# Paired softmax inverses, triangles by GpSimd in the second batch, zero matmuls between early steps, and new figures and random turns in the planner of an attention and feed-forward kernel

## The chip, the cores and the metric

One core of a Trainium2 chip runs one program. The metric is the device time of one execution in microseconds (us). PE is the matrix engine, DVE the vector engine, ACT the scalar engine, POOL is GpSimd, SP issues transfers.

## What is computed

```
scores = q @ k.T / 8, kept where key < 4 (sinks) or 0 <= query - key < 128, else -1e9
a   = exp(scores - max);  a = a / (sum(a) + 1e-9)
x   = a @ v, heads side by side                # 4 batches, 8 heads, 768 positions, 64 wide: x is 4 x 768 x 512
u   = x + ((x.T @ U) @ V).T                    # U 768 x 32, V 32 x 768: mixes the positions
out = u + relu(u @ w1) @ w2                    # w1 512 x 2048, w2 2048 x 512
```

q, k and v are fp32 in memory; U, V, w1 and w2 are fp64, which the kernel reads as raw 64-bit words and narrows itself; the two scalars (sinks and window) are integers.

## The kernel before, in words

The work is written as steps (`Plan.add`, `Plan.any`): each has an engine or a choice of engines with a cost in us for each, the buffers it reads and writes, and a priority. When all steps are there, `Plan.order` builds the program's order: `forward` simulates the engines with these costs and hands out steps, `backward` computes new priorities from the end, eleven passes in turn, and the order of the pass that came out shortest by the planner's own figures is emitted. Each engine then runs its instructions strictly in that order; a semaphore wait holds everything behind it on the same engine.

The stages, in the order of the data:

- **Start.** `sink_attention_mixer` (before `Fast`) runs eight matmuls on zeros (`spin`, L1320), loads the two scalars, builds masks on DVE and POOL, and issues the first transfers: q and k of two pairs of heads, and the 64-bit words of U, V (two halves) and the first w1 block into four `big` buffers (L1332).
- **Attention of batches 0 and 1** goes by pairs of heads (`attend_pair`). For each of three blocks of 128 queries and each head PE computes a score block into a bank of PSUM (L652); DVE scales, masks and takes the row minimum of the negated block (`soften`, L704, with an accumulator read); ACT takes the exponential and the row sum (L707). `normalise` adds 1e-9 to the three sums of a head (L715, ACT or DVE, the planner picks), DVE takes the reciprocal (L718), and POOL, ACT or DVE scale the probabilities (L729, L727, L730). PE transposes them (L745); the transposed blocks get two triangles: the part from the previous key block by a DVE multiplication with a mask straight out of PSUM (L754), the own block by a copy (L467 or L468) and a POOL affine_select (L770). PE multiplies with v (L675).
- **Attention of batches 2 and 3** goes head by head (`scores`, `values`), in a split fp32r form; there both triangles are POOL selects (L767 and L770), because `transposes` gets `whole=False`.
- **Mixing**: sums over positions, the product with V, and `u` split into a high and a low part (`uh`, `ul`; L982, L474).
- **Feed-forward** (`ffn`): 16 blocks of 128 hidden units by two halves of 384 positions by four batches. A block is 12 matmuls of 384 columns (L1006, L1007, L1008), a relu (ACT or DVE, `hh`), a low part (`hl`, L1017, DVE), and 9 matmuls of 512 columns (L1027). In batch 0 the weights come in beside it: `weights` narrows each of 32 half blocks by seven operations on DVE, ACT and POOL (`narrow_steps`, L99 to L108), then writes a high part (L467) and a low part (L474, `w`). The attention of the next batch runs beside the feed-forward of this one.

PE, DVE, ACT and POOL take their steps from one list, so one changed cost moves instructions everywhere. Banks of PSUM are a ring of eight: a step that writes a bank waits until all readers of its last content are done.

## Time and profile before

| | us |
|---|---|
| three runs | 753.15, 753.34, 753.82; median 753.34 |
| profiled execution, first to last instruction (its span) | 750.5 |
| between that span and the median of the runs | 2.84 |
| PE busy in the span | 727.3 (97%) |
| DVE, ACT, POOL busy | 454.3, 341.4, 194.0 |

The profile lists the span of the profiled execution and no other time of it; what lies around the span is put at the 2.84 us between it and the median. Busy time of PE is the union of its matmuls, which overlap, so it counts some waiting as work; waits are to be read from the steps between starts.

### The profile page before, as it was taken

What the parts mean: (1) busy time and instruction counts of PE and PEld (TensorE: products, weight loads), DVE (VectorE), ACT (ScalarE), POOL (GpSimd) and SP (SyncE); (2) the same over time, 40 slices, a digit from 0 to 9 for tenths busy, and PEclk for the clock granted to TensorE, in tenths of its full rate; (3) what the DMA queues carried; (4) which work ended last, traced back from release to release, by engine and by line L of the source; (5) the groups of instructions that cost most, each with busy time, mean ns of one, the idle gap of its engine ahead of it and who ended that gap; (6) DMA issues with size and microseconds to landing.
All of it is one profiled execution on the core that took longest, in us unless ns stands there. A gap on an engine that the chain in (4) does not pass through costs nothing.

```text
span 750.5 us, 11587 instructions
## 1 busy us (share of the span) xinstructions
PE 727.3 (97%) x4012; PEld 629.2 (84%) x4012; DVE 454.3 (61%) x1168; ACT 341.4 (45%) x977; POOL 194.0 (26%) x316
## 2 busy tenths in 40 slices
PE   7989999999998999999999999999999999999997
PEld 5557777777787999999899899999999989889895
DVE  7999889798999577667751287675653131112111
ACT  6986475775874445555541164564441111111110
POOL 4652030421521263263510043544401000000000
PEclk9999999999999999999999999999999999999999
DMA  7466758755795378563575468760276536524752
GB/s 261 150 197 226 261 182 302 258 184 205 240 296 223 124 244 278 177 209 117 167 241 183 153 194 256 231 211 1 71 263 227 169 135 237 199 76 138 267 176 96
DMA packets 43780, 146.84 MB, mean 196 GB/s; under 512 B 5440, under 2 KB 12224, under 8 KB 34240
## 3 DMA queue, kind: packets, MB, share of 16 engines
q1 hardware_dynamic: 43424, 145.62, 57.7%
q8 instruction: 33, 0.54, 0.3%
q10 hardware_dynamic: 288, 0.39, 0.2%
q14 instruction: 35, 0.29, 0.1%
HBM read 116.37 MB, written 29.62 MB: 195 GB/s over the span
## 4 chain that ended last, share of the span: by engine, by line
PE 84%; DVE 11%; ACT 1%; issue 1%; DMA 1%; POOL 0%; SPq 0%; DVEq 0%; ACTq 0%
PE bank L1027 33%; PE bank L1006 12%; PE bank L1007 11%; PE bank L1008 11%; PE bank L793 3%; PE bank L745 2%; PE bank L652 2%; PE bank L675 2%; DVE nr L104 2%; PE bank L695 2%; PE bank L696 2%; DVE w L474 1%; DVE bank L106 1%; PE bank L906 1%; DVE p L704 1%
## 5 line engine op out<-in xcount | busy, mean ns | idle before, releaser
L1027 PE MATMUL bank<-w,hh 128*128 128x512 f32 x768 | 246.2, 402 | 1.2 <-ACT hh L1014 0.6
L1017 DVE SCALAR_TENSOR_TENSOR hl<-bank,hh 128x384 fp32r<-128x384 f32 x128 | 70.9, 554 | 186.9 <-ACT hh L1014 186.1
L1006 PE MATMUL bank<-ul,w 128*128 128x384 f32 x512 | 178.5, 349 | 0.8 <-ACT w L467 0.7
L1007 PE MATMUL bank<-uh,w 128*128 128x384 f32 x512 | 174.0, 340 | 1.8 <-DVE w L474 1.8
L1008 PE MATMUL bank<-uh,w 128*128 128x384 f32 x512 | 173.1, 338 | 0.0
L1014 ACT ACTIVATE hh<-bank 128x384 fp32r<-128x384 f32 x121 | 59.3, 490 | 236.6 <-PE bank L1008 235.9
L1027 PEld LDWEIGHTS bank<-w,hh 128*128 128x128 f32 x768 | 139.6, 189 | 24.5 <-issue 1.4
L1027 PE MATMUL bank<-w,hl 128*128 128x512 f32 x384 | 151.8, 395 | 2.3 <-DVE hl L1017 2.3
L1006 PEld LDWEIGHTS bank<-ul,w 128*128 128x128 f32 x512 | 96.3, 188 | 12.1 <-issue 3.4
L1007 PEld LDWEIGHTS bank<-uh,w 128*128 128x128 f32 x512 | 96.4, 188 | 8.6 <-DVE w L474 3.7
L1008 PEld LDWEIGHTS bank<-uh,w 128*128 128x128 f32 x512 | 96.2, 188 | 0.0
L1027 PEld LDWEIGHTS bank<-w,hl 128*128 128x128 f32 x384 | 72.2, 188 | 20.8 <-DVE hl L1017 3.6
L707 ACT ACTIVATE p<-p,ms 128x132 f32<-128x132 f32 (+1 forms) x144 | 69.9, 486 | 33.4 <-DVE ms L704 32.9
L704 DVE CUSTOM_DVE_ANT_0 p<-bank,mask 128x132 f32<-128x132 f32 (+1 forms) x144 | 54.3, 401 | 13.3 <-PE bank L696 10.8
L476 POOL TENSOR_TENSOR p<-p 128x256 f32<-128x256 f32 (+1 forms) x26 | 21.7, 836 | 131.0 <-ACT p L707 130.3
L476 POOL TENSOR_TENSOR ul<-xT,uh 128x384 fp32r<-128x384 f32 x14 | 14.4, 1050 | 146.0 <-ACT uh L467 146.0
L467 ACT COPY tb<-bank 64x384 f32<-64x384 f32 x31 | 14.7, 474 | 40.0 <-PE bank L793 40.0
L729 POOL TENSOR_TENSOR p<-p,r 128x396 f32<-128x396 f32 x27 | 24.2, 898 | 32.4 <-DVE r L718 26.0
L474 DVE TENSOR_TENSOR xT<-bank,tb 64x384 f32<-64x384 f32 x32 | 17.5, 548 | 23.1 <-ACT tb L467 22.8
L770 POOL TENSOR_SCALAR_AFFINE_SELECT oph<-oph 128x384 fp32r<-128x384 f32 (+1 forms) x48 | 27.4, 572 | 12.8 <-ACT oph L467 10.2
L745 PE MATMUL bank<-ident,p 128*128 128x128 f32 x144 | 24.9, 278 | 3.4 <-POOL p L729 2.2
L770 POOL TENSOR_SCALAR_AFFINE_SELECT opl<-opl 128x384 fp32r<-128x384 f32 (+1 forms) x48 | 26.1, 544 | 7.4 <-ACT opl L467 4.1
(187 smaller groups left out, 1137.7 us busy)
## 6 DMA issues: line engine op xcount, KB each, us to landing
w<-wd SPq DMA_DIRECT2D x60, 1024.0 KB, 4.9
big<-in_w_dram SPq DMA_DIRECT2D x32, 512.0 KB, 4.2
wd<-w SPq DMA_DIRECT2D x14, 1024.0 KB, 4.4
big<-xd SPq DMA_DIRECT2D x33, 256.0 KB, 3.2
qkraw<-in_k_dram SPq DMA_DIRECT2D x32, 198.0 KB, 5.3
qkraw<-in_q_dram SPq DMA_DIRECT2D x32, 192.0 KB, 4.0
out_dram<-big SPq DMA_DIRECT2D x24, 256.0 KB, 2.2
v_raw<-in_v_dram SPq DMA_DIRECT2D x16, 192.0 KB, 3.2
```

The lines of the kernel that those rows point to most:

```text
L474: ways = {"DVE": (dve(n), lambda: nc.vector.tensor_tensor(dst(), a(), b(), op), pool)}
L476: ways["POOL"] = (gps(n), lambda: nc.gpsimd.tensor_tensor(dst(), a(), b(), op), True)
L704: add("DVE", dve(wd), lambda: nc.vector.tensor_tensor_reduce(p()[:, u, NS + lo:], st()[:, :wd], self.mask[:, min(qb, 2), lo:], -0.125, 3.0 ...
L707: add("ACT", act(wd) + 0.22, lambda: nc.scalar.activation(p()[:, u, NS + lo:], p()[:, u, NS + lo:], AF.Exp, bias=sm()[:, u:u + 1], scale=-1.0,
L745: nc.tensor.transpose(tr()[:, u * P:(u + 1) * P], p()[:, u, SW + NS:], self.ident)
L770: add("POOL", 0.126 + CH * 0.914e-3, lambda t=t: nc.gpsimd.affine_select(as_(t()[:, :, 1, :]), f32(t()[:, :, 1, :]), [[0, NBLK], [1, P]], ...
L1006: nc.tensor.matmul(ph()[:, :CH], wh, ul()[:, d, :], start=d == 0, stop=False)
L1007: nc.tensor.matmul(ph()[:, :CH], wl, uh()[:, d, :], start=False, stop=False)
L1008: nc.tensor.matmul(ph()[:, :CH], wh, uh()[:, d, :], start=False, stop=d == NC - 1)
L1014: self.plan.any({"ACT": (act(CH), lambda: nc.scalar.activation(hh(), ph()[:, :CH], AF.Relu)), "DVE": (dve(CH), lambda: nc.vector.tensor_sc ...
L1017: add("DVE", dve(CH), lambda: nc.vector.scalar_tensor_tensor(hl(), ph()[:, :CH], 0.0, f32(hh()), ALU.max, ALU.subtract), r=(ph, hh), w=(hl ...
L1027: nc.tensor.matmul(acc[k](), a()[:, sl], w()[:, m, :], start=not begin and i == 0 and j == 0, stop=i == n - 1 and j == 2)
```

## The change

- `attend_pair` keeps the row sums of both heads in one tile and takes the inverse once for six columns (`inverse`), in place of twice for three. Both engines stay allowed for the 1e-9.
- `transposes` gets `late`, true for batch 1 to 3: there the triangle of the previous key block is a POOL select from the copied own block, and the DVE multiplication is left out. Batch 0 keeps it.
- 12 matmuls on zeros at the start in place of 8, and 30 more as steps of the lowest priority that the planner puts where it finds PE idle in the first attention. Each writes a bank of its own.
- Planner: after the eleven passes two seeded random disturbances of the priorities (`shaken`), each kept if its span by the planner's figures is shorter; the cost of a matmul, of a transfer and of the first four loads is replaced (`mm`, `RATE`, `EARLY`, a step without duration on SP), and the paired score step is 0.06 us dearer.
- The ring for descriptors that software writes is set to 1024 bytes.

```diff
-NSPIN = 8
+NSPIN = 12
+NIDLE = 30
+TURNS = 4
+SEEDS = (300012, 300026,)
+RATE = 360e3
+EARLY = (0.55, 1.5, 2.5, 3.8)
...
+        for seed in SEEDS:
+            best = self.shaken(seed, best)
...
+    def shaken(self, seed, best):
+        rnd = random.Random(seed)
+        by, t, width = rnd.choice((0.3, 1.0, 3.0, 8.0)), rnd.uniform(-20.0, 260.0), rnd.choice((20.0, 60.0, 300.0))
...
+        for s in self.steps:
+            g = rnd.gauss(0.0, by)
+            if t <= s.start < t + width:
+                s.prio += g
+        for _ in range(TURNS):
...
+            if self.span < best[0] - 1e-6:
+                best = self.span, [s.prio for s in self.steps]
+            self.backward()
...
-    return k * max(n + (44 if n > CH else 34), 262) / 2400.0
+    return k * max(n * 1.085 + 6, 262) / 2400.0
...
-lat=nbytes / 330e3, prio=prio)
+lat=nbytes / RATE, prio=prio)
...
             self.early.pop(0)
+            self.plan.add("SP", 0.0, lambda: None, w=(raw,), lat=-EARLY[NBIG - 1 - len(self.early)], prio=-1e6)
...
-        sms = [self.ms(), self.ms()]
+        sm = self.ms()
...
-            add("PE", 0.105 + wd / 600.0, mms, ...)
+            add("PE", 0.165 + wd / 600.0, mms, ...)
...
+        r = self.inverse(sm, 2 * NBLK, t0)
         for i in range(2):
-            self.normalise(b, 2 * pr + i, half, t0 + i, ps[i], sms[i], self.sinks[b])
-            ts += self.transposes(half, t0 + i, ps[i], True, self.opl if i else self.oph)
+            self.normalise(b, 2 * pr + i, half, t0 + i, ps[i], r, i * NBLK, self.sinks[b])
+            ts += self.transposes(half, t0 + i, ps[i], True, self.opl if i else self.oph, b > 0)
...
-        if whole:
+        if whole and not late:
             tri = ...
             add("DVE", dve(nu * P), lambda: nc.vector.tensor_tensor(...))
...
         for t in res:
-            if not whole:
+            if late:
                 add("POOL", 0.126 + nu * P * 0.914e-3, lambda t=t: nc.gpsimd.affine_select(...))
...
+        zero = nc.const_aps.tensor(0.0, [P, P], F32)
+        for _ in range(NIDLE):
+            box = self.bank()
+            self.plan.add("PE", 0.22, lambda box=box: nc.tensor.matmul(box()[:, :P], zero, zero, start=True, stop=True),
+                          w=(box,), prio=1e6)
```

The order that comes out moves on every engine. Three places follow. The names are tiles (`p` and `qkraw` hold probabilities, `bank` a bank of PSUM, `nr` a narrowing buffer, `oph` and `opl` the transposed probabilities of the two heads); the lines of the change are 39 to 50 higher than before.

DVE behind the branch at the start, before (L101 is the second step of U's narrowing, whose first is on ACT; L704 is the first softening):

```order
L1340 TENSOR_LOAD sc_flag
L1341 COMPARE_AND_BRANCH
L101 TENSOR_SCALAR nr<-nr 128x192
L704 ISA p_176,ms<-bank_162,mask 128x132
L704 ISA ms 128x1
L704 ISA qkraw,ms<-bank_163,mask 128x132
```

and now:

```order
L171 TENSOR_SCALAR mask<-m_back,sc_val 128x2x128
L1389 TENSOR_LOAD sc_flag
L1390 COMPARE_AND_BRANCH
L743 ISA p_180,ms<-bank_166,mask 128x132
L743 ISA ms 128x1
L743 ISA qkraw,ms<-bank_167,mask 128x132
```

U's narrowing left the head of DVE; its first step (L105) stands behind fourteen softenings now, on DVE itself.

PE in the first attention, before: scores of the third pair, then the transposes of the first:

```order
L652 MATMUL bank_167<-kh,qs 128x132
L652 MATMUL bank_168<-kh,qs 128x260
L652 MATMUL bank_169<-kh,qs 128x260
L652 MATMUL bank_162<-kh,qs 128x260
L652 MATMUL bank_163<-kh,qs 128x260
L745 MATMUL bank_164<-ident,p_176 128x128 x3
L745 MATMUL bank_165<-ident,qkraw 128x128 x3
```

and now (L1174 are the zero matmuls):

```order
L690 MATMUL bank_172<-kh,qs 128x260
L1174 MATMUL bank_168<-const-float32-0.0 128x128
L1174 MATMUL bank_169<-const-float32-0.0 128x128
L1174 MATMUL bank_173<-const-float32-0.0 128x128
L1174 MATMUL bank_170<-const-float32-0.0 128x128
L788 MATMUL bank_166<-ident,p_180 128x128 x3
L788 MATMUL bank_168<-ident,qkraw 128x128 x3
```

Four of the thirty stand right ahead of the first transposes, three others further ahead; the rest stand behind them, and all thirty stand in nine groups of 3, 4, 8, 3, 5, 1, 2, 3 and 1, from behind the scores of the second pair to ahead of the first x transposes (L950).

DVE in the attention of batch 1, first pair, before:

```order
L104 SCALAR_TENSOR_TENSOR nr<-big_111,nr 128x512
L754 TENSOR_TENSOR oph<-bank_169,tri 128x2x128
L754 TENSOR_TENSOR opl<-bank_168,tri 128x2x128
L474 TENSOR_TENSOR qkraw<-qkraw 128x3x128
L718 RECIPROCAL r<-r 128x3 x2
```

and what POOL has for that pair now:

```order
L513 TENSOR_TENSOR p_180<-p_180 128x3x128
L811 AFFINE_SELECT oph<-oph 128x2x128
L811 AFFINE_SELECT opl<-opl 128x2x128
L513 TENSOR_TENSOR qkraw<-qkraw 128x3x128
L814 AFFINE_SELECT oph<-oph 128x3x128
L814 AFFINE_SELECT opl<-opl 128x3x128
```

The two multiplications of a pair left DVE, and two selects stand ahead of the two that POOL had.

## Rows read from the trace of the kernel before

**Rows 1.** The page, part 1: busy time, share of the span, instructions.
```profile
PE 727.3 (97%) x4012; PEld 629.2 (84%) x4012; DVE 454.3 (61%) x1168; ACT 341.4 (45%) x977; POOL 194.0 (26%) x316
```

**Rows 2.** Windows: stretch, length; busy of PE, PEld, DVE, ACT, POOL; PEclk, DMA share, GB/s.
```profile
10.00:85.00 75.00, 65.16 (x397) 44.11 (x394) 72.78 (x219) 58.28 (x186) 34.21 (x53) 1.00 0.62 208
85.00:235.00 150.00, 145.84 (x814) 115.77 (x812) 136.19 (x350) 98.56 (x267) 39.94 (x52) 1.00 0.70 241
```

**Rows 3.** Waits of PE, 10 to 85 us: us in total, times, longest.
```profile
PE bank L745 <- POOL p L729: 2.2, 2, 1.5
PE bank L745 <- POOL qkraw L729: 2.0, 4, 0.7
```

**Rows 4.** Waits of PE, 60 to 240 us: us in total, times, longest.
```profile
PE bank L1027 <- DVE hl L1017: 2.3, 2, 2.1
PE bank L1007 <- DVE w L474: 1.8, 6, 0.3
PE bank L1006 <- ACT w L467: 0.7, 2, 0.4
...
PE bank L745 <- POOL qkraw L729: 0.3, 1, 0.3
```

**Rows 5.** Timeline of the start: start us, length us, engine, instruction, idle before.
```profile
0.84 3.75 PE L1320 MATMUL spin<-const-float32-0.0 128*128 128x128 f32 x16 [0.84 <-PEq L1385]
...
6.05 2.54 PE L652 MATMUL bank<-first0k,first0q 64*128 64x132 f32 x12 [1.45 <-DVE m_ck L161]
...
7.06 0.38 ACT L100 ACTIVATE nr<-big 128x192 bf16<-128x192 bf16 x1 [4.76 <-DMA big<-in_U_dram]
...
7.54 0.21 DVE L101 TENSOR_SCALAR nr<-nr 128x192 bf16<-128x192 bf16 x1 [1.24 <-ACT nr L100]
7.67 0.29 DVE L704 CUSTOM_DVE_ANT_0 p<-bank,mask 128x132 f32<-128x132 f32 x1
...
11.40 1.37 PE L652 MATMUL bank<-kh,qs 64*128 64x132 f32 x12 [1.06 <-DVE ms L704]
```

**Rows 6.** Weight loads by source line: duration ns min/median/max, first and last start.
```profile
L1320 PEld LDWEIGHTS spin<-const-float32-0.0 x16: 287/333/334, 0.8 to 4.0; 128*128 128x128 f32 x16
...
L652 PEld LDWEIGHTS bank<-kh,qs x24: 183/187/188, 11.4 to 14.6; 64*128 64x128 f32 x24
```

**Rows 7.** Groups by line and form, whole span: count, busy us, mean ns, idle before.
```profile
L104 DVE SCALAR_TENSOR_TENSOR nr<-big,nr 128x512 uint16<-128x512 uint16 x32 | 22.6, 705 | 0.9
...
L718 DVE RECIPROCAL r<-r 128x3 f32<-128x3 f32 x64 | 9.9, 164 | 1.6 <-ACT r L715 1.3
...
L754 DVE TENSOR_TENSOR oph<-bank,tri 128x384 f32<-128x384 f32 x8 | 4.4, 548 | 1.4 <-POOL psink L733 1.2 <-ACT oph L467 0.2
...
L754 DVE TENSOR_TENSOR oph<-bank,tri 128x256 f32<-128x256 f32 x8 | 3.3, 413 | 0.9 <-PE bank L745 0.5 <-ACT oph L467 0.3
...
L767 POOL TENSOR_SCALAR_AFFINE_SELECT oph<-oph 128x384 fp32r<-128x384 f32 x16 | 8.3, 520 | 0.9 <-ACT oph L467 0.9
```

**Rows 8.** Timeline of DVE where batch 0 hands over to batch 1.
```profile
228.21 4.04 DVE L982 TENSOR_TENSOR xT<-xT,bank 128x384 f32<-128x384 f32 x8
...
232.77 0.56 DVE L1017 SCALAR_TENSOR_TENSOR hl<-bank,hh 128x384 fp32r<-128x384 f32 x1
```

**Rows 9.** Timeline of PE at the same place.
```profile
235.73 0.44 PE L1006 MATMUL bank<-ul,w 128*128 128x384 f32 x1 [0.45 <-ACT w L467]
236.50 0.45 PE L1007 MATMUL bank<-uh,w 128*128 128x384 f32 x1 [0.33 <-DVE w L474]
...
236.96 0.34 PE L1006 MATMUL bank<-ul,w 128*128 128x384 f32 x1
237.13 0.34 PE L1007 MATMUL bank<-uh,w 128*128 128x384 f32 x1
```

**Rows 10.** Timeline, POOL and DVE, at U's narrowing.
```profile
15.70 0.93 POOL L729 TENSOR_TENSOR p<-p,r 128x396 f32<-128x396 f32 x1 [0.78 <-DVE r L718]
15.84 1.00 DVE L104 SCALAR_TENSOR_TENSOR nr<-big,nr 128x192 uint16<-128x192 uint16 x1
```

More of the change, by code (lines that the diff above doesn't have):

```diff
@@ L1 @@
+import random
 import struct
@@ L287, in order, with put_back @@
                 self.backward()
-        for s, p in zip(self.steps, best[1]):
-            s.prio = p
+        for seed in SEEDS:
+            best = self.shaken(seed, best)
+        self.put_back(best[1])
         self.forward()
         return sorted(self.steps, key=lambda s: (s.start, s.n))
+    def put_back(self, prios):
+        for s, p in zip(self.steps, prios):
+            s.prio = p
+    def shaken(self, seed, best):
+        rnd = random.Random(seed)
+        by, t, width = rnd.choice((0.3, 1.0, 3.0, 8.0)), rnd.uniform(-20.0, 260.0), rnd.choice((20.0, 60.0, 300.0))
+        if rnd.random() < 0.2:
+            t += 280.0
+        self.put_back(best[1])
+        self.forward()
+        for s in self.steps:
[3 more added lines that the diff above has]
+        for _ in range(TURNS):
+            try:
+                self.forward()
+            except ValueError:
+                break
+            if self.span < best[0] - 1e-6:
+                best = self.span, [s.prio for s in self.steps]
+            self.backward()
+        return best
     def backward(self):
@@ L322, in backward @@
                 sync = self.SYNC[p.eng] if p.eng != e else (0.0 if e == "PE" else SAME)
-                p.ready_b = max(p.ready_b, s.back + p.lat + sync + (1.95 if p.eng == "SP" else 0.0) if whole else s.back - p.dur)
+                p.ready_b = max(p.ready_b, s.back + max(p.lat, 0.0) + sync + (1.95 if p.eng == "SP" else 0.0) if whole else s.back - p.dur)
                 if not p.left:
@@ L389, in forward @@
             end = t + s.dur + s.lat
-            if e == "SP":
+            if e == "SP" and s.lat < 0.0:
+                end = -s.lat
+                dma = max(dma, end - 1.3)
+            elif e == "SP":
                 dma = max(dma, t + s.dur + 0.65) + s.lat
@@ L482, in fn @@
             self.nc.sync.dma_start(d, s)
-        self.plan.add("SP", 0.5 if rows == P else 0.65, fn, r=r, w=((box, part),) if box else (), lat=nbytes / 330e3, prio=prio)
+        self.plan.add("SP", 0.5 if rows == P else 0.65, fn, r=r, w=((box, part),) if box else (), lat=nbytes / RATE, prio=prio)
     def narrow(self, src, n, prio, dst=()):
@@ L705, in soften, with inverse, normalise @@
             p()[:, u, NS + lo:], st()[:, :wd], self.mask[:, min(qb, 2), lo:],
-            -0.125, 3.0e38, ALU.add, ALU.min, sm()[:, u:u + 1]), r=(st,), w=((p, u), (sm, u)), prio=t0)
+            -0.125, 3.0e38, ALU.add, ALU.min, sm()[:, j:j + 1]), r=(st,), w=((p, u), (sm, j)), prio=t0)
         add("ACT", act(wd) + 0.22, lambda: nc.scalar.activation(
-            p()[:, u, NS + lo:], p()[:, u, NS + lo:], AF.Exp, bias=sm()[:, u:u + 1], scale=-1.0,
-            accum_out=sm()[:, NBLK + u:NBLK + u + 1]), r=((sm, u),), w=((p, u), (sm, NBLK + u)), prio=t0)
-    def normalise(self, b, h, half, t0, p, ms, psink):
+            p()[:, u, NS + lo:], p()[:, u, NS + lo:], AF.Exp, bias=sm()[:, j:j + 1], scale=-1.0,
+            accum_out=sm()[:, n + j:n + j + 1]), r=((sm, j),), w=((p, u), (sm, n + j)), prio=t0)
+    def inverse(self, ms, n, t0):
         nc, add = self.nc, self.plan.add
         r = self.rr()
-        sm = lambda: ms()[:, NBLK:]
-        self.plan.any({"ACT": (0.2, lambda: nc.scalar.activation(r(), sm(), AF.Copy, bias=1e-9)),
+        sums, out = lambda: ms()[:, n:2 * n], lambda: r()[:, :n]
+        self.plan.any({"ACT": (0.2, lambda: nc.scalar.activation(out(), sums(), AF.Copy, bias=1e-9)),
                        "DVE": (0.4, lambda: nc.vector.scalar_tensor_tensor(
-                           r(), sm(), 1e-9, sm(), ALU.add, ALU.max), True)}, r=(ms,), w=(r,), prio=t0)
-        add("DVE", 0.09, lambda: nc.vector.reciprocal(r(), r()), w=(r,), prio=t0)
+                           out(), sums(), 1e-9, sums(), ALU.add, ALU.max), True)}, r=(ms,), w=(r,), prio=t0)
+        add("DVE", 0.09, lambda: nc.vector.reciprocal(out(), out()), w=(r,), prio=t0)
+        return r
+    def normalise(self, b, h, half, t0, p, r, j, psink):
+        nc, add = self.nc, self.plan.add
         kept = lambda: p()[:, :, SW:]
-        by = lambda: r().unsqueeze(2).broadcast_to([P, NBLK, SW])
+        by = lambda: r()[:, j:j + NBLK].unsqueeze(2).broadcast_to([P, NBLK, SW])
         u0 = 1 if half == 0 else 0
@@ L736, in normalise, with transposes @@
                       r=(p,), w=((psink, (half, h)),), prio=t0)
-    def transposes(self, half, t0, p, whole, own=None):
+    def transposes(self, half, t0, p, whole, own=None, late=True):
         nc, add = self.nc, self.plan.add
@@ L761, in transposes @@
         else:
-            self.copy(CH, top, v3, psum=True, r=(tr,), w=((res[0], 1),), prio=t0)
+            self.copy(CH, lambda: as_(top()), v3, psum=True, r=(tr,), w=((res[0], 1),), prio=t0)
+        if not whole:
             self.tt(CH, lambda: res[1]()[:, :, 1, :], v3, lambda: f32(top()), ALU.subtract, pool=False,
@@ L805, in attend @@
         p, sm = self.scores(half, t0, *qk)
-        self.normalise(b, h, half, t0, p, sm, self.sinks[b])
+        self.normalise(b, h, half, t0, p, self.inverse(sm, NBLK, t0), 0, self.sinks[b])
         self.values(h, half, t0, self.transposes(half, t0, p, False), v, xT)
```

19 lines of the change are left out of this document (10 added, 9 removed).

## The prediction

> **What bounds the kernel now.** Read the page first: PE is busy for 97% of the span [rows 1], so nearly all the span is matmuls that the change doesn't touch, and only PE's gaps can be won. The windows say where they lie. From 10 to 85 us, in batch 0's attention, PE works 65.16 of 75 us and DVE 72.78: DVE is the bound and PE has 9.84 us of slack. From 85 to 235 us, in batch 0's feed-forward with batch 1's attention beside it, PE works 145.84 of 150 and DVE 136.19, 91% [rows 2]: PE leads, and DVE is so full that PE is late whenever DVE is. The granted clock is 1.00 in both, the 2.4 GHz level. The table's span less busy PE leaves 23.2 us; these two stretches hold 14.0 of it, and the rest lies at the start, at the end where the output goes out, and thinly between.
>
> The waits name the causes. In the first stretch the largest are transposes (L745) that wait for POOL's scaling of the probabilities (L729), 4.2 us in 6 waits [rows 3]. From 60 to 240 us nine groups of waits hold 7.6 us in 16 waits (the first three and the last are shown), most released by DVE, or by ACT in a chain with DVE [rows 4]. The longest, 2.1 us, is at the handover from batch 0 to batch 1: DVE runs eight multiplications L982, 4.04 us, before the `hl` at 232.77 on which PE stands [rows 8].
>
> Listed waits are too short. At the handover PE's step from 235.73 to 236.50 is 0.77 us where consecutive steps are 0.17 (236.96 to 237.13), so 0.60 is lost and 0.33 is listed: up to 0.27 hides in one wait, as matmul records overlap [rows 9].
>
> The sum is made against this execution's span, 750.5 us. The median of the runs lies 2.84 above it, and I add that at the end.
>
> **A. The start: -0.5 us.** The spin ran from 0.84 to 4.59, 16 records of 0.234 us; four more matmuls are 8 records, 1.9 us, so it ends at 6.47. The first scores began at 6.05, when DVE's mask was ready, so they can come 0.4 late. DVE's first softening was at 7.67, right behind L101, for which DVE sat idle 1.24 us, as L101 waited for ACT's L100 on U's transfer [rows 5]. L101 is gone from there. Twelve score records took 2.54 us, so the first bank is full some 0.4 after 6.47, and DVE can start 0.8 earlier. The ends are -0.8 (DVE bound, as in all that follows) and +0.4 (PE's last score bound); I take -0.5, since DVE is the full engine. The loads of the spin took 333 ns against 187 for the scores from 11.4 us on [rows 6], which is the lower level (1.2 GHz) and then the higher; PE had done nothing before the spin.
>
> The Trainium skill, "TensorE: Matmul & The Clock Gate", Part 1, says that the lower rate is the default and that sustained activity releases it. These rows agree so far, and by that rule a longer spin would let the scores run at full rate and bring A to its end of -0.8.
>
> **B. DVE's work before the feed-forward: +0.5 us.** By the order lists DVE has 168 instructions ahead of the fourth `ul` of batch 0, and had 171. In it are one more weight half (about four operations of DVE at up to 0.705, the row of L104, so 2.8 us at most), eight fewer reciprocals (8 x 0.164 = 1.3) [rows 7], and copies that went to ACT. Against this stands a new wait: one inverse for two heads comes when the second head's sums are there, so the first head's scaling, for which PE already waits [rows 3], starts about one softening later, 0.2 to 0.4 us, in eight pairs of batch 0; nothing else in DVE's queue waits there. Ends: -1 (copies won, no delay felt) and +2.
>
> **C. The waits from 60 to 240 us: -5.5 us.** From batch 1's DVE go 16 triangles, 4.4 + 3.3 = 7.7 us, 16 reciprocals, 2.6 us [rows 7], and four relus, 2.2 us at the 0.56 of a like operation [rows 8]; five first narrowing steps come, up to 3.5 us at L104's duration. That is 9 to 12.5 us less before the handover; I take 11, since a few copies move to ACT too. DVE's load falls from 91% to about 83%. The pool of waits is 7.6 listed and 16 x 0.27 = 4.3 hidden, 11.9 at most. Of it the three at the handover are 2.1 + 0.45 + 0.33 [rows 8, 9] and 0.8 hidden, 3.7. There the eight L982 still stand together ahead of the same `hl`, so lighter DVE helps only by arriving earlier: I give back 1.8, half. Of the other 8.2 a bit under half, 3.7, because some are plain latency from DVE to PE, which a lighter DVE doesn't shorten. Ends: 0 (all are latency) and -11.9.
>
> **D. The zero matmuls: +0.3 us.** Thirty take two records each, at the higher clock about half of the spin's 0.234 each: 30 x 0.234 = 7.0 us of PE [rows 5, 6]. They lie in the 9.84 us of slack, so most cost nothing. But each needs a free bank and stands in order on PE, ahead of transposes and scores that DVE awaits. Ends: 0 and +7.0.
>
> **E. POOL's selects: +0.4 us.** Sixteen more at 0.520 [rows 7] are 8.3 us on POOL, which works only 39.94 of 150 us there [rows 2]; that slack covers them. PE's products with v now wait for POOL rather than DVE, with work queued behind on POOL. What can also cost is DVE held up: one L104 of 192 columns took 1.00 us, from 15.84, beside a POOL scaling that took 0.93 [rows 10], where 512 columns usually take 0.705 [rows 7]. Ends: 0 and +8.3 (each select holds DVE for its whole length, on the path). I take the low value, since of DVE's operations shown in these stretches L104 is the one stretched, and only 32 of it exist.
>
> The Trainium skill, "SBUF — State Buffer", "Who interferes with whom", says that DVE and GpSimd share a port pair as an exclusive lock, against a DVE operation with two SBUF inputs among others, and that the loser blocks fully. The stretched L104 has two such inputs and agrees. By the rule the softenings, `hl` and the L982, which read one input from PSUM, stay free; it speaks against the move only where an L104 or a like operation meets a select, which is the second rival below.
>
> **F. The rest: -0.2 us.** 16 ACT additions fewer; the 1e-9 was on ACT all along, since the reciprocals waited for L715 there [rows 7]. From 240 us on PE has hardly any gap. Later batches are reordered: +-0.7. The descriptor ring is not used: the page lists hardware queues alone.
>
> **Sum:** -0.5 + 0.5 - 5.5 + 0.3 + 0.4 - 0.2 = -5.0; span 745.5, time 748.3 us. Neither the half of C nor the shuffled order can be read from a row; they make the range.
>
> **The rivals.**
> 1. *DVE's saving comes back in full.* If from 85 us on PE's waits all go, C is -11 and the time 742.8. For it: DVE at 91% and PE waiting on `w` and `hl` alone. Against: the eight L982 stay together.
> 2. *Little comes back.* Either the waits on `w` are latency, or the selects hold up L104 and others: of the 16 selects some 11 may meet such an operation, and if half of these lie on the path at 0.5 each, 2.7 us are lost from C. The time is about 751.0. The Trainium skill's page on SBUF, named under E, has this as its rule. For it: the stretched L104. Against: POOL is idle most of the stretch.
> 3. *The change doesn't do what it says, or trades evenly.* The 1e-9 was with ACT already and the zeros need no power from a clock that stands at 1.00; what is left is another order with the same waits: 752 to 755.
> 4. *Slower: the zeros.* They hold banks of the ring of eight and PE's queue. If DVE must sit idle in front of a softening or a triangle because transposes came late behind zeros, the first stage, which has DVE as its bound, grows by up to 7.0 us, with C reduced to -4: 756.5. It decides once those idles of DVE pass about 5 us in sum. For it: four zeros stand right ahead of the first transposes. Against: 0.234 us each, in PE's slack.
>
> **How the numbers follow.** Forecast 0.50; rival 1 0.12; rival 2 0.20; rival 3 0.08; rival 4 0.10. A measurement of this kernel tells about 0.2%, 1.5 us, from no change. The forecast and the first two rivals are below 751.8: faster 0.82; same 0.08; slower 0.10. Around the forecast the likeliest case spans 746 to 750.5 (C from -3.5 to -7.5). The range goes from 742.0, which takes in half of rival 1 and more, to 753.0, past rival 2 and into rival 3; outside remain under 0.05 below, and 0.04 of rival 3 and rival 4's 0.10 above.
>
> **What the changed profile would show.** For A: the first softening before 7.6 us and weight loads near 187 ns at the first scores; wrong if it starts at 7.7 or later. B: the first feed-forward matmuls within 1 us of before. C: PE's slack from 85 to 235 down from 4.2 to about 2, the wait on `hl` at the handover down from 2.1 to about 1, DVE busy some 11 us less by then, the L754 sixteen and the POOL selects L767 and their kin sixteen more. If the slack stays at 4 the forecast is wrong. D: thirty zeros between 10 and 45 us with no new DVE idle before softenings. E: L104's mean near 705; above 800, rival 2. Slower in the first 85 us by over 3 us would make rival 4.

## The result and the profile after

The changed kernel ran at 744.42 to 748.17 us in six runs, median 746.6, against 753.17 for the kernel before beside it: a ratio of 0.9902, 95% interval 0.9882 to 0.9923, which is 7.4 us (5.8 to 8.9); the two medians lie 6.6 apart. The forecast was 748.3, 5.0 us faster, with a range from 742.0 to 753.0. The number held. The experiments below show that its largest term did not: the largest part of the gain that the traces can place comes from something the prediction never looked at.

The two stretches of [rows 2], as they are in the changed kernel's profiled execution (span 745.9 us):

```profile
10.00:85.00 75.00, 70.40 (x451) 52.74 (x452) 69.30 (x209) 58.76 (x185) 32.54 (x52) 0.98 0.64 210
85.00:235.00 150.00, 145.32 (x811) 114.69 (x809) 133.85 (x326) 99.24 (x262) 48.30 (x67) 1.00 0.71 241
```

In the second, PE's slack is 4.68 us where it was 4.16, though DVE has 2.3 us less to do and POOL 8.4 us more. DVE worked 91% of this stretch and works 89% now, where C expected 83%. By the prediction's own test ("if the slack stays at 4 the forecast is wrong") part C is wrong. PE's waits from 60 to 240 us, the answer to [rows 4] (us in total, times, longest):

```profile
PE bank L1071 <- DVE hl L1061: 1.8, 2, 1.6
PE bank L1018 <- DVE t L1001: 1.2, 1, 1.2
PE bank L933 <- DVE xT L936: 0.9, 1, 0.9
PE bank L1050 <- ACT w L504: 0.5, 1, 0.5
PE bank L1051 <- DVE w L511: 0.3, 1, 0.3
...
```

The many short waits for `w` are fewer, the wait for `hl` at the handover is 1.6 us in place of 2.1, and new waits in the mixing (L1018, L933) stand beside it.

The start, beside [rows 5]:

```profile
0.84 5.46 PE L1369 MATMUL spin<-const-float32-0.0 128*128 128x128 f32 x24 [0.84 <-PEq L1434]
6.36 1.37 PE L690 MATMUL bank<-first0k,first0q 64*128 64x132 f32 x12
...
7.11 0.30 DVE L743 CUSTOM_DVE_ANT_0 p<-bank,mask 128x132 f32<-128x132 f32 x1 [0.88 <-PE bank L690]
```

The spin is longer, the scores follow it at once and at the full rate (12 records in 1.37 us, 2.54 before), and DVE starts at 7.11 where it started at 7.67. The first feed-forward matmul, before and then now, came 3.75 us later, where the prediction wanted it within 1 us as the mark of B:

```profile
65.16 0.35 PE L1006 MATMUL bank<-ul,w 128*128 128x384 f32 x1
```

```profile
68.91 0.34 PE L1050 MATMUL bank<-ul,w 128*128 128x384 f32 x1
```

To see where time is won, count the `hl` instructions, 128 in all, and compare when the same one starts in two kernels. The 4th lies at 85.93 us in the kernel before, the 28th (just behind the handover) at 239.84, the last at 741.26. Each column is the difference to that, in us, from the profiled executions:

```
kernel                          4th     28th    128th
changed                        -0.70   -0.89   -4.51
changed, again (e1)            -0.44   -1.73   -5.49
no zeros (e2)                  -1.58   -4.29   -9.37
first seven zeros (e9)         -1.79   -4.69   -9.75
no random turns (e4)           +0.19   +0.64   +1.42
other random turns (e7)        -1.10   -0.35   -0.59
old work, new planner (e8)     +3.24   +7.71   +4.02
before, lighter DVE (e5)       +0.08   -1.56   -0.35
```

From the 28th to the last `hl` the changed kernel wins another 3.6 us, in a stretch for which the prediction had 0.2. The end of it, from the 88th `hl` (570.9 us) to the last, has no attention left and holds 40 blocks: each of the twelve kernels built from the changed source wins 1.84 us there against the kernel before, whatever its order, and the kernel before with less DVE work (e5) wins 0.00. Here is one block of the feed-forward at 653 us, from its first matmul to the first of the next, in the timeline of PE of the kernel before:

```profile
653.21 0.34 PE L1006 MATMUL bank<-ul,w 128*128 128x384 f32 x1
653.38 0.34 PE L1007 MATMUL bank<-uh,w 128*128 128x384 f32 x1
...
657.43 0.34 PE L1006 MATMUL bank<-ul,w 128*128 128x384 f32 x1
```

and of the changed kernel:

```profile
653.83 0.34 PE L1050 MATMUL bank<-ul,w 128*128 128x384 f32 x1
654.00 0.34 PE L1051 MATMUL bank<-uh,w 128*128 128x384 f32 x1
...
658.01 0.34 PE L1050 MATMUL bank<-ul,w 128*128 128x384 f32 x1
```

The same 21 matmuls in the same order take 4.22 us and then 4.18, with no wait in either. Over all blocks that the next block follows with no other matmul between (51 in each kernel, left out one of 6.58 us before and two of 4.30 and 4.60 now) the means are 4.226 and 4.180, and they hardly vary (4.21 to 4.23; 4.18 in all). Most of it is in the steps from one 384-column matmul to the next, which became shorter from 0.1767 to 0.1733 us; those from one 512-column matmul to the next went from 0.2346 to 0.2326. Where the blocks stand free this is measured. If the blocks that other work interrupts gain as much, 128 times 0.046 is **5.9 us**, an estimate, and most of the gain.

### The profile page after: what moved, and what is told of

Read it like the earlier page. It is cut to its first block, busy times and chain, and to the rows that moved or that the text cites. A ratio compares the mean times of both kernels' runs of the same rounds, so it can differ in the third digit from the quotient of the medians.

```text
span 745.9 us, 11704 instructions
## 1 busy us (share of the span) xinstructions
PE 729.3 (98%) x4080; PEld 634.1 (85%) x4080; DVE 447.0 (60%) x1130; ACT 343.2 (46%) x974; POOL 198.3 (27%) x329
## 4 chain that ended last, share of the span: by engine, by line
PE 84%; DVE 7%; ACT 4%; DMA 3%; issue 1%; POOL 1%; SPq 0%; ACTq 0%; DVEq 0%; POOLq 0%
PE bank L1071 34%; PE bank L1050 12%; PE bank L1051 11%; PE bank L1052 11%; PE bank L837 3%; PE bank L788 2%; DMA xd<-first1k 2%; PE bank L690 2%; PE bank L714 2%; PE bank L734 2%; PE bank L735 2%; DVE bank L112 1%; ACT p L746 1%; DVE xT L1026 1%; PE spin L1369 1%
## 5 line engine op out<-in xcount | busy, mean ns | idle before, releaser
L1050 PE MATMUL bank<-ul,w 128*128 128x384 f32 x512 | 176.6, 345 | 1.0 <-ACT w L504 0.5
L1058 ACT ACTIVATE hh<-bank 128x384 fp32r<-128x384 f32 x125 | 61.3, 490 | 229.9 <-PE bank L1052 229.3
L513 POOL TENSOR_TENSOR p<-p 128x256 f32<-128x256 f32 (+1 forms) x25 | 19.5, 781 | 91.0 <-ACT p L746 90.3
L772 POOL TENSOR_TENSOR p<-p,r 128x396 f32<-128x396 f32 x26 | 22.1, 850 | 36.2 <-DVE r L757 20.0
L814 POOL TENSOR_SCALAR_AFFINE_SELECT oph<-oph 128x384 fp32r<-128x384 f32 (+1 forms) x48 | 25.9, 540 | 6.9 <-DVE opl L511 3.7
L746 ACT ACTIVATION_READ_ACCUMULATOR p<-p,ms 128x1 f32 x144 | 27.3, 189 | 0.0
```

Source lines behind the costliest of these rows:

```text
L513: ways["POOL"] = (gps(n), lambda: nc.gpsimd.tensor_tensor(dst(), a(), b(), op), True)
L746: add("ACT", act(wd) + 0.22, lambda: nc.scalar.activation(p()[:, u, NS + lo:], p()[:, u, NS + lo:], AF.Exp, bias=sm()[:, j:j + 1], scale=-1.0,
L772: "POOL": (0.82, lambda: nc.gpsimd.tensor_tensor(kept(), kept(), by(), ALU.mult), True),
L814: add("POOL", 0.126 + CH * 0.914e-3, lambda t=t: nc.gpsimd.affine_select(as_(t()[:, :, 1, :]), f32(t()[:, :, 1, :]), [[0, NBLK], [1, P]], ...
L1050: nc.tensor.matmul(ph()[:, :CH], wh, ul()[:, d, :], start=d == 0, stop=False)
L1058: self.plan.any({"ACT": (act(CH), lambda: nc.scalar.activation(hh(), ph()[:, :CH], AF.Relu)), "DVE": (dve(CH), lambda: nc.vector.tensor_sc ...
```

## The experiments

### The changed kernel again, and its zeros and its spin

```diff
 # e1: nothing changed
```

> The changed kernel as it is, beside the next three on one chip. Its profiled execution shows the granted clock at 0.50 from 50.7 to 54.0 us (mean 0.996) and ran 745.9 us between first and last instruction; three other executions had spans of 742.4 to 743.5. Theory P (the prediction's: the gain is in the stretch from 60 to 240 us, where DVE is lighter; zero matmuls and spin are worth about nothing): ratio to the kernel before 0.990, 746. Theory K (the gain is mostly a matter of TensorE's clock): executions in which the clock stays at 1.00 in that place are 3 us shorter than those in which it falls, so two groups of times, near 744.8 and near 747.9.

Measured: 747.0 us (746.59 to 747.44), ratio 0.9914 (0.9901 to 0.9927). The clock fell again, at the same place. Stretches of this run, with the columns of [rows 2]:

```profile
44.00:50.00 6.00, 3.94 (x28) 2.28 (x28) 5.82 (x12) 5.97 (x23) 4.06 (x7) 1.00 0.81 257
50.00:52.00 2.00, 1.66 (x11) 1.14 (x13) 1.55 (x4) 2.00 (x5) 2.00 (x4) 0.63 0.04 8
52.00:54.00 2.00, 2.00 (x13) 1.11 (x10) 1.79 (x4) 0.74 (x3) 0.08 (x1) 0.52 0.00 0
```

TensorE works 3.9 of 6 us ahead of 50 us, and then runs at the lower level (0.50, 1.2 GHz) for 3.4 us. The last zero matmul ends at 35 us. All five runs of this set are near 747, with a mean granted clock of 0.993 to 0.996. Of the first six, three were near 748 (0.996) and three near 745 (0.999 twice, 0.995 once). So theory K's two groups are there, and but for one run the clock goes with them; a trace with the fall exists for the first group alone.

```diff
-            self.plan.add("PE", 0.22, lambda box=box: nc.tensor.matmul(box()[:, :P], zero, zero, start=True, stop=True),
+            self.plan.add("PE", 0.22, lambda: None,
```

> The changed kernel with the order of its instructions held and the thirty zero matmuls not issued. Theory P: PE's slack takes them, so the time stays within 1 us of the changed kernel's (0 to -0.5). Theory K: without them TensorE falls to the half rate somewhere between 10 and 50 us, visible in the granted clock, and the time rises by 1 to 4 us over the changed kernel's. Rival Z (the zeros stand in the way of transposes that DVE awaits): 1 to 4 us faster than the changed kernel.

Measured: 744.13 us (743.31 to 744.35), ratio 0.9877 (0.9863 to 0.9892): 2.9 us faster than the changed kernel beside it, whose runs it doesn't meet. That is the time of rival Z. The clock did fall without the zeros, as theory K had it:

```profile
8.00:12.00 4.00, 1.42 (x14) 1.02 (x13) 2.69 (x19) 3.54 (x17) 1.41 (x2) 0.99 1.05 380
12.00:16.00 4.00, 4.00 (x24) 2.92 (x22) 3.63 (x19) 2.85 (x10) 2.44 (x4) 0.58 0.84 271
...
50.00:52.00 2.00, 1.76 (x19) 1.30 (x19) 1.63 (x4) 2.00 (x6) 1.99 (x4) 1.00 0.00 0
```

It stands at 0.58 from 12 to 16 us, after PE worked 1.42 of 4 us, but it doesn't fall at 50. The 4th `hl` comes 1.1 us sooner than in e1, the 28th 2.6 and the last 3.9. That looks like zeros in the way of DVE's work, but another run takes that reading away. DVE has the same 1130 instructions in the same order in all of these kernels, so they can be compared one by one. The run without selects (e6, below) issues all thirty zeros, differs from e1 only behind 104 us, where the first select of batch 1 stands, and its traced execution has no fall at 50:

```profile
44.00:50.00 6.00, 3.94 (x28) 2.28 (x28) 5.81 (x12) 5.97 (x23) 4.05 (x7) 1.00 0.75 250
50.00:52.00 2.00, 1.76 (x19) 1.30 (x19) 1.63 (x4) 2.00 (x6) 1.98 (x4) 1.00 0.03 8
```

When four of DVE's instructions start, in us after the same one in e2, where they lie at 15.8, 37.8, 50.5 and 57.1 us:

```
                                 57th    141st   177th   189th
seven zeros, no fall (e9)       -0.65    -0.23   -0.22   -0.22
thirty, no fall (e6)            -0.76    +0.27   -0.01   -0.01
thirty, fall at 50 (e1)         -0.64    +0.39   +0.10   +1.13
thirty, fall at 50 (changed)    -0.70    +0.33   +0.04   +0.87
```

The thirty zeros cost DVE something on the way, but from 44 us on they leave it 0.2 us behind the run with seven. The 1.1 us at the 4th `hl` are the fall of the clock at 50 us, in a stretch that DVE bounds. The other 2.8 us come later. At the handover, DVE waits 0.43 us behind a transfer that was slow to land (`xd<-first1k`, 6.45 us from its issue, 5.93 in e2), and one narrowing step of DVE takes 1.31 us beside a subtraction of POOL, where it takes 0.29 in e2. At 371 and 549 us e1 loses another 1.3 us, the larger part while ACT waits 3.3 us for another landing of `xd<-first1k`. So rival Z's number came true, and its mechanism is worth 0.2 us in these traces. Whether the zeros make the fall at 50 or the other losses likelier is open: the fall is in two of the three traced executions of this order with thirty zeros and a spin of twelve (e6 is the third), and in e8, which has none, the clock falls at 48.6.

```diff
-NSPIN = 12
+NSPIN = 8
```

> The changed kernel with the order held and eight matmuls in the spin, as before, in place of twelve. Theory P (part A worth 0.5, mostly from U's narrowing leaving DVE's head): DVE's first softening at 6.8 to 7.2 us as in the changed kernel (7.11) and the time within 0.5 us. Theory K: the first twelve score records take 2.3 to 2.6 us instead of 1.37, DVE falls behind by 0.5 to 1 us, and the time rises by that.

Measured: 745.93 us, ratio 0.9900 (0.9879 to 0.9922), runs from 743.73 to 749.1, which tells it apart from nothing. Its trace answers one question:

```profile
0.84 3.75 PE L1369 MATMUL spin<-const-float32-0.0 128*128 128x128 f32 x16 [0.84 <-PEq L1434]
6.24 1.37 PE L690 MATMUL bank<-first0k,first0q 64*128 64x132 f32 x12 [1.65 <-DVE m_ck L167]
```

With eight matmuls in the spin the first scores run at the full rate too, 0.19 us later than in the kernel before, where they ran at half. So the longer spin isn't needed for the full rate; DVE started at 6.96, sooner than behind the longer spin. This execution lost clock twice (0.63 of full from 12 to 16 us, 0.57 from 52 to 56), though it issues all thirty zeros: they don't hold the clock by themselves.

```diff
+NKEEP = 7
...
+        left = itertools.count()
...
-            self.plan.add("PE", 0.22, lambda box=box: nc.tensor.matmul(...),
+            self.plan.add("PE", 0.22, lambda box=box: nc.tensor.matmul(...) if next(left) < NKEEP else None,
```

> The changed kernel with its order held and the first seven of the thirty zero matmuls issued, the other 23 not. With none, the granted clock fell to 0.50 from 12 to 15 us, after PE had been idle for 2.6 us ahead of the third pair's scores; with all thirty it stayed at 1.00 there and DVE reached the feed-forward 1.1 us later than with none. Theory D2 (zeros help where they keep the clock, and cost where they stand ahead of work that DVE awaits): no fall at 12 us, and 0.5 to 2 us faster than with none, 742 to 743.6. Rival (a fall of 3 us in DVE's stretch costs nothing): the same as with none, 744.

Measured: 743.4 us (742.66 to 743.69), ratio 0.9866 (0.9848 to 0.9883), the **lowest median** of this study, below all runs of both kernels. In its profile the clock doesn't fall before 737 us:

```profile
12.00:16.00 4.00, 3.87 (x34) 2.90 (x30) 4.00 (x25) 3.07 (x11) 2.58 (x5) 1.00 0.90 294
...
50.00:52.00 2.00, 1.97 (x20) 1.34 (x20) 1.60 (x4) 2.00 (x5) 1.78 (x3) 1.00 0.00 0
```

Against no zeros at all it wins 0.2 us at the 4th `hl` and 0.7 in the medians; the intervals overlap, so D2 and its rival are not told apart.

### The order

```diff
-SEEDS = (300012, 300026,)
+SEEDS = ()
```

> The changed kernel without the two seeded disturbances of the planner's priorities; everything else as changed, order planned anew. Theory P: the structural parts carry the gain, so within 1.5 us of the changed kernel. Rival S (the gain is an order that happened to come out well): 2 to 5 us above the changed kernel, 749 to 752.

Measured: 754.84 us, ratio 1.0022 (1.0012 to 1.0032): slower than the kernel before, and 8 us from the changed one, with all other parts of the change in it. Rival S holds, by more than it asked.

```diff
-SEEDS = (300012, 300026,)
+SEEDS = (62, 67, 108, 176, 185)
```

> The changed kernel with five other seeds for the random turns in place of the two; by the planner's own figures the order is as good as the changed one. Theory P (the structure carries the gain and the first order without turns was an unlucky one): 745 to 749. Rival S (each order is a draw, which the planner's figures do not rank): it can come out anywhere from 745 to 756; a time over 750 bears S out.

Measured: 751.57 us, ratio 0.9960 (0.9940 to 0.9980). The planner rates this order like the changed one; the chip sets them 5 us apart. Rival S again. (Its traced execution has the clock at 0.50 from 232.6 us for 3.4 us; all ten runs lie above 749.5, at a mean clock of 0.994 to 0.999.)

```diff
-NSPIN = 12
-NIDLE = 30
-SEEDS = (300012, 300026,)
+NSPIN = 8
+NIDLE = 0
+SEEDS = (1, 2, 4, 16, 67, 84, 85, 123, 148, 176)
...
-        r = self.inverse(sm, 2 * NBLK, t0)
         for i in range(2):
+            r = self.inverse_of(sm, 2 * NBLK, i * NBLK, t0)
-            ts += self.transposes(..., self.opl if i else self.oph, b > 0)
+            ts += self.transposes(..., self.opl if i else self.oph, False)
...
```

> The work of the kernel before (eight spins, no zeros, an inverse for each head, batch 1's triangles on DVE) under the new planner: its figures for matmuls and transfers and ten random turns. Theory P (the lighter DVE is needed): 751 to 755. Rival S: the planner's part alone gives the gain or most of it, 745 to 750.

Measured: 755.14 us, ratio 1.0002 (0.9981 to 1.0022). The planner's part alone gives nothing, and rival S doesn't hold for it; the time is just above theory P's 751 to 755. This run has the short blocks of 4.180 us as well, and loses them again by the 28th `hl`, 7.7 us late. Its mean clock is 0.989, with 0.69 from 8 to 16 us and 0.81 from 16 to 30, so lost clock is a part of that. Its two runs at a mean clock of 0.998 took 752.2 and 752.9, and the kernel before took 752.2 to 752.6 at that clock in the same set.

### Lighter DVE, lighter POOL

```diff
 # e5, on the kernel before, in batch 1
-            add("DVE", dve(nu * P), lambda: nc.vector.tensor_tensor(
+            add("DVE", dve(nu * P), lambda: None if skip else nc.vector.tensor_tensor(
...
+                    if b > 0:
+                        mv = ts[i]()[:, lo // 2:lo // 2 + hi - lo, 1, :]
```

> The kernel before with its order held, and the sixteen multiplications with the triangle in the attention of batch 1 (L754) not issued: DVE loses 7.7 us of work between 85 and 228 us and nothing else moves. Work left out: the part of the probabilities from the previous key block in batch 1 is not masked; the product with v reads the own block in its place, with as many matmuls. Theory P (PE's waits between 60 and 240 us come from a full DVE): 3 to 7 us faster than the kernel before, with the handover's wait on hl shorter. Rival S (the gain of the change is its order; lighter DVE alone is worth little): within 1.5 us of the kernel before.

Measured: 751.74 us (750.94 to 752.39), ratio 0.9966 (0.9951 to 0.9982): 1.4 to 3.7 us of the 7.7 taken from DVE. By the trace the 28th `hl` is 1.56 us sooner. The wait for `hl` at the handover is 2.0 us, where it was 2.1. The result lies between the two theories: the mechanism of C exists, and a fifth to a half of what DVE is spared comes back, where C reckoned with a half (5.5 of 11).

```diff
 # e6, on the changed kernel: the new selects of batch 1 aren't issued
-                add("POOL", 0.126 + nu * P * 0.914e-3, lambda t=t: nc.gpsimd.affine_select(
+                add("POOL", 0.126 + nu * P * 0.914e-3, lambda t=t: None if whole else nc.gpsimd.affine_select(
...
+                    if b > 0:
+                        mv = ts[i]()[:, lo // 2:lo // 2 + hi - lo, 1, :]
```

> The changed kernel with its order held, and the sixteen new POOL selects of batch 1 not issued. Work left out: the same mask as in the run on the kernel before, with the product reading the own block. Theory P (part E: 0.4): within 1 us of the changed kernel. Rival L (the selects hold DVE up, or PE waits for them): 2 to 5 us faster than the changed kernel, 742 to 745.

Measured: 746.48 us, ratio 0.9892 (0.9861 to 0.9923), which is the changed kernel's. The selects cost nothing that can be measured; rival L falls. DVE's instructions bear it out: at 57 us and again at 209 us they are 0.2 us behind those of e9, which has the selects and seven zeros.

```diff
 # e11, on the changed kernel without zeros: one hl of DVE, at the handover
...
+        s = order.pop(low)
+        need = max(order.index(d) for d in s.deps)
+        order.insert(max(need + 1, at[3]), s)
...
```

> The changed kernel, order held, no zeros, and one instruction of DVE moved: the hl on which PE waits at the handover from batch 0 to batch 1 stands ahead of the last five of the eight multiplications with a bank. Theory P as in part C (the eight in front of hl are what PE waits for): the 1.6 us wait on hl goes and 1 to 2 us are gained against the run without zeros. Rival T (DVE is the bound through the handover, and the next weight half w comes when its work is done): the wait on hl goes and PE waits as much longer for w, so within 0.5 us.

Measured: 746.47 us, ratio 0.9906 (0.9886 to 0.9927), runs from 743.0 to 748.61, so no gain. PE's waits from 220 to 240 us, first in the run without zeros (e2):

```profile
PE bank L1071 <- DVE hl L1061: 1.6, 1, 1.6
PE bank L1050 <- ACT w L504: 0.4, 1, 0.4
PE bank L1051 <- DVE w L511: 0.3, 1, 0.3
```

and here:

```profile
PE bank L1060 <- ACT w L504: 2.4, 1, 2.4
PE bank L1061 <- DVE w L511: 0.3, 1, 0.3
```

The wait for `hl` is gone, and PE waits 2.0 us longer for `w` instead. The 28th `hl` starts 4.15 us before the one in the kernel before; without the move it was 4.29. Rival T holds: moving `hl` alone gains nothing, as PE then waits for `w`, which comes out of the same queue of DVE. The spread of these runs (mean clock 0.988 to 0.996) shows that times near 748 come without any zeros, too.

### What the order without turns loses

```diff
 # e10, on e4: for batches 2 and 3
+        whole = lambda: nc.vector.tensor_tensor(kept(), kept(), by(), ALU.mult)
-        self.plan.any({"ACT": (NBLK * 0.3, scale),
+        self.plan.any({"ACT": (NBLK * 0.3, whole if b > 1 else scale),
```

> The changed kernel without random turns, order held, but in batches 2 and 3 the scaling of the probabilities that its order gives to ACT (nineteen times three instructions) is one DVE instruction at the same place. In that order PE waited four times, at 291, 321, 468 and 497 us, for such a scaling, and lost about 1.0 us each by the steps between starts; the changed order has no such wait. Theory W (the turns gain by avoiding named waits, these four among them): the four waits go and the time falls by 3 to 5 us against the order without turns, to 750 to 752. Rival (another wait takes their place, or PE is behind for other reasons): within 1.5 us of 754.8.

Measured: 758.29 us, ratio 1.0064 (1.0049 to 1.0080): 3.5 us slower, where theory W had 3 to 5 faster. (Its traced execution has the clock at 0.50 for 6.8 us from 234 us; the run at a mean clock of 0.999 took 758.26 all the same.) PE's waits from 280 to 510 us, in e4 and then here:

```profile
PE bank L788 <- ACT p L770: 1.7, 4, 0.4
```

```profile
PE bank L789 <- DVE p L771: 4.2, 4, 1.1
```

The four waits stayed and grew, so the engine that scales was not their cause. One step further back stands what was. The first of the four in e4, rows of POOL, DVE, ACT and PE:

```profile
289.05 2.10 POOL L513 TENSOR_TENSOR kl<-qkraw,kh 128x792 fp32r<-128x792 f32 x1 [0.56 <-DVE kh L505]
289.31 2.26 DVE L511 TENSOR_TENSOR p<-p 128x384 f32<-128x384 f32 x1
291.49 0.23 DVE L757 RECIPROCAL r<-r 128x3 f32<-128x3 f32 x2
291.68 1.89 ACT L770 ACTIVATE p<-p,r 128x132 f32<-128x132 f32 x6 [1.77 <-DVE r L757]
292.14 0.92 PE L788 MATMUL bank<-ident,p 128*128 128x128 f32 x3 [0.43 <-ACT p L770]
```

DVE's addition takes 2.26 us, ends 0.42 after POOL's subtraction, and the reciprocal, the scaling and PE's transposes all queue behind it. The same pair (POOL 2.09, DVE 2.25, 0.26 apart) stands at 318.5, 465.4 and 495.0 us, and in e7 DVE's addition takes 2.25 us four times too. In the changed kernel no addition does, though other instructions of DVE meet the same (see C below).

```diff
 # e12, on e4: kl of POOL in four parts
+            for i in range(0, nk, 198):
+                sl = slice(i, i + 198)
+                nc.gpsimd.tensor_tensor(kl()[:, sl], kr()[:, sl], f32(kh()[:, sl]), ALU.subtract)
```

> The changed kernel without random turns, order held, but POOL's subtraction that makes kl (128x792, 2.09 us) is issued as four of 128x198. In the run without turns, at the four places where PE waited for a scaling, DVE's addition p<-p (128x384) had started 0.26 us after such a kl on POOL and took 2.25 us where it takes 0.6 on average elsewhere, ending 0.4 us after POOL did; with the scaling moved to DVE the four waits stayed, behind the same addition at 2.25. Theory X (DVE is held up by the POOL instruction for its whole length, rival 2's mechanism in another place than the selects): the four additions fall below 1.2 us, the waits on the scaling go or fall below 0.1, and the time falls by 2 to 4 us against the run without turns (ratio 1.0022), to a ratio of 0.997 to 0.9995. Rival Y (POOL's four parts follow each other without letting DVE in, or the addition waits for something else): the additions stay at 2.2 us or more and the ratio within 0.001 of 1.0022.

Measured: 752.44 us, ratio 0.9976 (0.9961 to 0.9992), against 1.0022 for the order without turns: 3.5 us. The first of the four places now:

```profile
290.12 3.56 POOL L645 TENSOR_TENSOR kl<-qkraw,kh 128x198 fp32r<-128x198 f32 x4 [0.56 <-DVE kh L505]
290.38 0.97 DVE L511 TENSOR_TENSOR p<-p 128x384 f32<-128x384 f32 x1
```

and the group of these additions by line and form (count, busy us, mean ns), first in e4, then here:

```profile
L511 DVE TENSOR_TENSOR p<-p 128x384 f32<-128x384 f32 x19 | 18.0, 948 | 2.4 <-ACT p L746 2.4
```

```profile
L511 DVE TENSOR_TENSOR p<-p 128x384 f32<-128x384 f32 x19 | 12.8, 676 | 2.4 <-ACT p L751 2.4
```

POOL is slower in parts (3.56 us for what took 2.10), and the kernel is faster. No such addition of DVE takes over 1.0 us any more. The four waits are gone from PE's list. Theory X holds, as predicted in size. It accounts for 3.5 of the 8 us between the order without turns and the changed one; where the rest goes was not traced.

The Trainium skill, "SBUF — State Buffer", "Who interferes with whom", has the rule for this: an exclusive port pair, and the later instruction blocks until the earlier one ends. The rows agree, DVE's addition reading both its inputs from SBUF and ending 0.42 us after POOL.

## Why the prediction held, and where it failed

**A, the start (-0.5): right.** DVE's first softening came 0.56 us sooner. With U's narrowing gone from the head of DVE a spin of eight is enough for it: there it came at 6.96. The prediction let a longer spin bring the full rate of the first scores, with the Trainium skill's "TensorE: Matmul & The Clock Gate", Part 1, beside it; they ran at the full rate with the short spin too (e3).

**B with D up to the feed-forward (+0.8, with A +0.3): wrong by its own mark, near by the 4th `hl`.** The first feed-forward matmul was to come within 1 us of before; it came 3.75 us later (2.6 in e9). The first blocks then follow each other faster, and the 4th `hl` came 0.4 to 0.7 us sooner, and 1.6 to 1.8 where the clock didn't fall at 50 us (e2, e6, e9). Which of B's terms was short was not tried.

**C (-5.5): wrong in size. The step that failed is "DVE's load falls from 91% to about 83%", and with it the half of PE's waits that was to go.** From the 4th to the 28th `hl` the changed kernel won 0.2 us in one execution and 1.3 in the other (2.7 and 2.9 in e2 and e9), of which 24 shorter blocks (0.046 each) are up to 1.1. From 10 to 235 us DVE works 5.8 us less, 208.97 before and 203.15 now, where C had 11. The triangles and the relus went as counted. But of the reciprocals eight left batch 1, not sixteen: up to the 28th `hl` 32 of three columns (5.1 us) became 16 of six (2.9 us) in batches 0 and 1 together, and B had counted batch 0's already. And one of the narrowing steps became dearer, 3.6 us in all, before and then now:

```profile
L101 DVE TENSOR_SCALAR nr<-nr 128x512 bf16<-128x512 bf16 x32 | 9.5, 295 | 0.0
```

```profile
L107 DVE TENSOR_SCALAR nr<-nr 128x512 bf16<-128x512 bf16 x32 | 13.1, 408 | 0.5 <-ACT nr L106 0.3
```

Two of the 32 make up 2.7 us of that. Each starts just behind a subtraction of POOL and ends just behind it. These are rows of POOL and DVE in the changed kernel:

```profile
197.50 1.91 POOL L513 TENSOR_TENSOR kl<-qkraw,kh 128x792 fp32r<-128x792 f32 x1 [0.40 <-DMA qkraw<-in_k_dram]
197.69 1.86 DVE L107 TENSOR_SCALAR nr<-nr 128x512 bf16<-128x512 bf16 x1
219.55 1.29 POOL L513 TENSOR_TENSOR xhl<-first1q,xhl 128x512 fp32r<-128x512 f32 x1 [6.99 <-ACT xhl L504]
219.59 1.40 DVE L107 TENSOR_SCALAR nr<-nr 128x512 bf16<-128x512 bf16 x1
```

The second lies at the handover, where this execution also waited 1.3 us for a transfer; the run with seven zeros has neither, and its 28th `hl` came 3.8 us sooner. Taking the triangles from DVE in the old order is worth 1.4 to 3.7 us of 7.7 (e5). Half the handover's wait was to go because DVE "arrives earlier"; it was 1.6 for 2.1, and where `hl` was put ahead of five of the eight multiplications PE waited for `w` instead (e11).

**D (+0.3, ends 0 and +7.0): right for what it names.** In the traces the thirty zeros keep DVE back by 0.2 us at the feed-forward's start (e6 beside e9). Without them the median is 2.9 us lower (e2). The two traced executions, 3.9 apart, put that down to a fall of the clock, to landings of transfers and to a DVE step beside POOL, not to zeros ahead of transposes; that rival 4's mechanism costs more than 0.2 is not shown. Nor is it shown that zeros hold the clock: the kernel before has none and stays at 1.00 from 12 to 16 us, and e3 has all thirty and falls there.

**E (+0.4): right.** L110, the L104 of before, takes 704 ns on average, with 192 columns 361 instead of 998 [rows 10], and without the selects nothing changes (e6). The mechanism named for rival 2, DVE held up by POOL, is real all the same, but POOL's subtractions do it and not its selects: on the narrowing steps under C, and for 3.5 us on additions in batches 2 and 3 in the order of e4 (e7 has the same rows), which the changed order happens to avoid.

**F (-0.2, +-0.7): wrong.** From the 28th `hl` on 3.6 to 3.8 us were won in the two traces. The 100 blocks there are 4.6 us of it by the cadence; the rest went the other way (e2 and e9 won 5.1 there).

So the forecast of 5.0 met 7.4 (6.5 in the repetition e1, by its ratio) by terms that don't match: an estimated 5.9 us of cadence stand where 5.5 of C stood. That the number held is luck. Without that term the changed kernel's work and order would be worth about 0.5 to 1.5 us, and the draws of the order (e4, e7, the changed one: 754.8, 751.6, 746.6 or 747.0 with the same work and the same cadence) range over 8 us, more than any part of the change.

**What remains open** is why the steps are shorter. All twelve profiles of kernels built from the changed source have blocks of 4.18 us whatever their order (e4, e7 and e8 too), and the two of kernels built from the source before (e5 is the other) have 4.23, e5 and e8 on one chip in one set. So neither the order nor the planner's search nor the chip is the cause. What the twelve share, and the two don't, is where the buffers lie. The built programs' memory maps have, in bytes within a partition:

```
            before                changed
ms          7 tiles, 32 apart     7 tiles, 64 apart
w0          45152                 29792      (15360 lower: the descriptor ring)
uh          189120, 195264        173984, 180128   (15136 lower)
ul          201408, 207552        186272, 192416   (15136 lower)
hh          213696, 215232        198560, 200096   (15136 lower)
hl          216768, 218304        201632, 203168   (15136 lower)
```

The sums of two heads in one tile make `ms` wider, so these tiles of the feed-forward move by 224 bytes against `w`. Before, `uh` and `ul`, which the 384-column matmuls stream, and `hh` and `hl`, the weights of the 512-column ones, start at multiples of 64, and now 32 past one; `w` is 32 past one in both. That the place of an operand sets the step is argued from this, not shown: a kernel before with seven wider `ms` tiles, and nothing else, would tell, and it wasn't tried.

## What to carry to other kernels

Compare the step of the steady loop in both traces to the nanosecond before looking at any wait: 1% of a step that runs all the time outweighs every wait on the list, and an unrelated buffer's size may have set it. When a planner orders a program, run several of its orders before crediting a change with the difference; here equal work spread over 8 us. When two kernels keep the order of an engine, compare its instructions one by one: here that showed a difference of 2.9 us in the medians to arise mostly elsewhere than at the part that was left out. And where DVE and GpSimd both read SBUF for long, look for an instruction that takes far more than its usual time and ends right behind the other engine's: cutting the long one in pieces won 3.5 us though it slowed that engine.

## What the runs showed of the hardware that was not expected

- The same matmul of 384 columns starts every 0.1767 us in one program and every 0.1733 in another, with nothing waiting, the clock at 1.00 in both.
- Four POOL subtractions of 198 columns took 3.56 us beside DVE where one of 792 took 2.10, and DVE's addition fell from 2.25 to 0.97.
- A DVE step on 128x512 bf16 that takes 0.295 us on average took 1.86 and 1.40 beside POOL subtractions.
- TensorE's clock fell to 0.50 for 3.4 us after 6 us in which PE worked 3.94 (e1), and in e6 and e9, with 3.94 and 3.95 of 6, it didn't fall.
- The first scores ran at half rate at 6.05 us (before) and at full rate at 6.24 (e3) behind the same spin.
